# A sliding-window attention with a gated MLP on one Trainium2 core: w_out loaded four consecutive rows per partition, w_in's blocks read with a stride of four

## The chip, the cores and the metric

The kernel runs on one core of a Trainium2 chip. The metric is the device time of one execution in microseconds. The core has five engines, which run on their own instruction streams and wait for each other by semaphores: PE (matrix multiply; its weight loads are listed apart as PEld), DVE (vector), ACT (activations), POOL (GpSimd) and SP (which here only issues DMAs). POOL issues the DMAs that load and cast the inputs. A few DMAs more come from SP and one from ACT. 16 DMA engines carry all of them.

## The reference, cut to what matters

```python
# attention: 8 batches, 8 heads, 576 positions, head size 64
scores = q @ k.T / sqrt(64)                 # only 0 <= row - col < 64 is kept
attn = softmax(scores)                      # rows
x = (attn @ v) as (8 * 576, 512)            # 4608 tokens, heads side by side
# MLP
h = x @ w_in                                # 512 -> 2048
g = h * cos(h)
out = g @ w_out                             # 2048 -> 512, float32
```

The order of the 2048 inner units is free: any permutation of w_in's columns leaves the output as it is, if w_out's rows are permuted alike.

## The kernel before, in words

**Stages.** The 4608 tokens are cut into nine token tiles of 512 (`mt` 0 to 8). The MLP of tile `mt` runs on PE while the attention that feeds the next tiles is worked in between, on all engines. Each token tile has a first part, h = x w_in in 16 blocks of 128 inner units (`ff`), each of four matmuls over the four pieces of the model dimension (`ks`), and a second part, out = g w_out. ACT takes the sine of h (shifted by pi/2), DVE multiplies it by h. The last three tiles (6 to 8) do the second part with seven products of halves in place of eight, for which sums of quarters of w_out are made beforehand (`sum_weights`).

**The weights.** `w_in_sb` is one SBUF tile of 128 partitions by 4 x 2048 in bfloat16: partition p holds row `ks * 128 + p` of w_in for the four `ks`, 2048 columns each. Four DMAs load it (`load_w_in`, line 208; steps `Lwi.0` to `Lwi.3`): piece i brings columns 512 i to 512 i + 511 of all four `ks`. Block `ff` is columns 128 ff to 128 ff + 127, so blocks 0 to 3 need piece 0 alone, 4 to 7 piece 1, and so on. `w_out_sb` is 128 partitions by 16 blocks by 512: partition p of block ff holds row 128 ff + p. Four DMAs load it (`load_w_out`, line 211; steps `Lwo.0` to `Lwo.3`), each with four rows of 2 KB per partition, which lie 128 rows apart in DRAM.

**The order of the work.** Up to the end of token tile 0 the order is written out by hand in the string `FIRST` (lines 51 to 71): each word is one step, and a step's instructions go to their engines in that order. Behind that a plan of due times (`at`, `pump`) does it. Each engine runs its own instructions strictly in order. The piece of `FIRST` that the change touches is this:

```python
"... w.0.1 w.1.1 c.1.1.a i.3.1 h.0.0.1 h.0.1.4 "
"tb n.2.1.p c.0.1.d Lwi.3 w.2.1 h.0.2.0 n.3.1.p v.0.1 S.0.0 Gm.11 w.3.1 S.0.1 h.0.3.3 Lwo.0 ..."
```

`h.g.f.bank` is `first_half` (line 455): inner blocks 2f and 2f + 1 for half g (256 tokens) of token tile 0, thus eight matmuls of 128x256 on line 460, with `ks` running innermost. `w.p.g` is a transpose of softmax weights on PE (line 409), `n.p.g.p` their normalisation on POOL (line 393), `S` the sine on ACT, `v` the values matmuls on PE. `Lwi.0` to `Lwi.2` stand well ahead of this piece, `Lwi.3` stands in it, behind `h.0.0` and `h.0.1`. From token tile 1 on the first part is line 496 (`first`), with matmuls of 128x512; the second part is line 479 for token tile 0, 747 for tiles 1 to 5 and 585 for 6 to 8.

**The waits.** Nobody writes the semaphore waits by hand. The tile layer under the kernel records what each instruction reads and writes of which tile, in the order of the program, and gives an instruction a wait wherever it finds that its bytes may overlap those of an earlier writer (or, for a write, of an earlier reader) on another engine or a DMA. Software DMAs take eight semaphores in turn; the four loads of w_in have the numbers 6, 7, 0 and 1, and a load first waits for the former user of its semaphore.

Of the kernel before, what the change touches and what calls it, by code (L numbers as in the profile page):

```python
# [74 lines left out]
def kernel(  # L75
# [9 lines left out]
    nc = tc.nc  # L85
# [5 lines left out]
    n_ff = d_ff // 128  # L91
# [14 lines left out]
    w_in_sb = const.tile([128, PAIRS, d_ff], BF16, name="w_in")  # L106
    w_out_sb = const.tile([128, n_ff, d_model], BF16, name="w_out")
    w_in_v = moe_w_in.rearrange("(a p) f -> p a f", p=128)
    w_out_v = moe_w_out.rearrange("(a p) f -> p a f", p=128)
    ident = const.tile([128, 128], BF16, name="ident")  # L110
    mask = const.tile([128, 3, 128], F32, name="mask")
    mask16 = const.tile([128, 6, 128], BF16, name="mask16")
# [4 lines left out]
    st = {}  # L117
# [3 lines left out]
    H_BANKS = [banks * 3 + [last] for *banks, last in (["O1", "X0", "X1", "S", "O0", "X0"], ["X1", "S", "X0", "O1", "O0", "S"])]  # L121
    BANKS = ("O1", "X0", "X1", "S", "O0")
    W_PARTS = 4
    half = MT // 2

    def bank(which, name):
        return ps.tile([128, 512], F32, tag=which, name=name)
# [53 lines left out]
    def load_chunk(name, b, c):  # L181
        if (name, b) not in st:
            st[name, b] = rows_tile(name)[:, 0:NB * d_model].rearrange("p (c x) -> p c x", c=NB)
        n = min(128, S - 128 * c)
        src = {"q": q, "k": k}[name][b, :, c * 128:c * 128 + n]
        nc.gpsimd.dma_start(out=st[name, b][0:n, c].rearrange("p (h d) -> p h d", h=H),  # L186
                            in_=src.rearrange("h p d -> p h d"))

    def load_v(b, c):
        n = 128 if c < 4 else 64  # L190
        vt = vtiles[b % 2][:n, 2 * c if c < 4 else 2 * c - 1]
        nc.gpsimd.dma_start(out=vt.rearrange("p (h d) -> p h d", h=H),  # L192
                            in_=v[b, :, c * 128:c * 128 + n, :].rearrange("h p d -> p h d"))
# [13 lines left out]
    def load_w_in(lo, hi):  # L207
        nc.gpsimd.dma_start(out=w_in_sb[:, :, lo:hi], in_=w_in_v[:, :, lo:hi])

    def load_w_out(lo, hi):  # L210
        nc.gpsimd.dma_start(out=w_out_sb[:, lo:hi], in_=w_out_v[:, lo:hi])

    def transposed(name, b, p):
        t_ps = ps_t.tile([128, S], BF16, tag="t", name=f"t{name}_ps")
# [240 lines left out]
    def first_half(g, f, which):  # L455
        st["h", g, f] = h_ps = bank(BANKS[which], "h_ps")
        for e in range(2):
            ff = 2 * f + e
            for ks in range(PAIRS):
                nc.tensor.matmul(out=h_ps[:, half * e:half * e + half], lhsT=w_in_sb[:, ks, ff * 128:ff * 128 + 128],  # L460
                                 rhs=st["xT", 0][:, ks, half * g:half * g + half], start=ks == 0, stop=ks == PAIRS - 1,
                                 skip_group_check=True)

# [10 lines left out]
    def second_part(q_, m, which=None):  # L474
        if q_ == 0:
            st["out", m] = bank(BANKS[which], "out_ps")
        n = n_ff // W_PARTS
        for ff in range(n * q_, n * q_ + n):
# [14 lines left out]
    def first(mt, ff, ks, start, stop):  # L493
        if start:
            st["h", ff] = bank(H_BANKS[mt == 1][ff], "h_ps")
        nc.tensor.matmul(out=st["h", ff], lhsT=w_in_sb[:, ks, ff * 128:ff * 128 + 128],  # L496
                         rhs=st["xT", mt][:, ks], start=start, stop=stop)

    def skewed(mt, ks, n):
        for ff in range(SKEW):  # L500
            first(mt, ff, ks, n == 0, n == PAIRS - 1)
# [107 lines left out]
    for i, (b, jobs, banks) in enumerate(bursts):  # L609
        t = T * (b - 1)  # L610
# [55 lines left out]
    for n in range(16):  # L666
        i, f = divmod(n, 4)
# [14 lines left out]
    def spread_first(lo, hi):  # L682
# [5 lines left out]
             "Lq1": lambda p: load_heads("q", 1, p, 1), "Lk1": lambda p: load_heads("k", 1, p, 1),  # L688
             "Lv0": lambda c: load_v(0, c), "Lv1": lambda c: load_v(1, c), "Lq2": lambda c: load_chunk("q", 2, c), "Lk2": lambda c: load_chunk("k", 2, c),
             "Lwi": lambda i: load_w_in(i * d_ff // W_PARTS, (i + 1) * d_ff // W_PARTS),  # L690
             "Lwo": lambda i: load_w_out(i * n_ff // W_PARTS, (i + 1) * n_ff // W_PARTS),
             "io": put_steps, "mk": put_masks, "mc": cast_masks,
             "tq": lambda p: tr_q(0, p), "tk": lambda p: tr_k(0, p), "Tq": lambda p: tr_q(1, p), "Tk": lambda p: tr_k(1, p),
             "pq": lambda p, engine: put_q(0, p, engine), "pk": lambda p, engine: put_k(0, p, engine),
# [6 lines left out]
             "n": lambda p, g, engine: g_norm(2 * p + g, engine), "w": lambda p, g: g_trans(2 * p + g),  # L701
             "c": lambda p, g, engine: g_put(2 * p + g, engine), "v": values_half, "x": put_x_half,
             "tb": sine_table, "tb2": exp_table, "h": first_half, "S": sine_half, "g": gate_half,
             "Gs": g_scores, "Gm": g_max, "Ge": g_exp, "Gi": g_inv, "Gn": g_norm, "Gw": g_trans, "Gc": g_trans,
             "Gp": g_put, "V": lambda p: values(1, p), "X": lambda p, engine: put_x(1, p, engine),
# [7 lines left out]
    for mt in range(1, n_mt):  # L713
# [7 lines left out]
        for ff in range(n_ff):  # L721
            for ks in range(PAIRS):
                if ff >= SKEW:
                    first(mt, ff, ks, ks == 0, ks == PAIRS - 1)
            h_ps = st.pop(("h", ff))
            sin = moe.tile([128, MT], F32, tag="sin", name="sin", bufs=4)
            if ff % 2 == 0:
                gt = moe.tile([128, 2, MT], BF16, tag="gT", name="gT", bufs=n_ff // 2 + 2)
                gT.append(gt)
            e = ff % 2  # L730
            nc.scalar.activation(sin, h_ps, AF.Sin, bias=math.pi / 2.0)  # L731
            if ff == n_ff - 1 and mt < B:
                exp_table()
            nc.vector.tensor_tensor(out=gt[:, e], in0=h_ps, in1=sin, op=ALU.mult)  # L734
            pump(base + ff)
# [51 lines left out]
```

## Time and profile before

| what | value |
|---|---|
| runs of the kernel before | 299.11, 299.21, 297.6 us (median 299.11) |
| the profiled execution's own time | 296.92 us |
| its span in the profile | 295.2 us |
| PE busy | 285.3 us, 97% of the span |
| PEld busy (beside PE) | 163.2 us |
| DVE, ACT, POOL busy | 230.3, 238.0, 209.7 us |
| software DMA queue | 100896 packets, 18.06 MB written |
| granted TensorE clock | 1.0 |

All times below are us from the start of the span. A matmul's duration in the profile holds its latency (379 ns for 128x512); in a row of matmuls one starts much sooner than the former ends, so how fast a row goes is read from its length by its count. In the tables of waits an engine's idle time is put down to what ended it. A DMA's "us to landing" is from its issue.

### The profile page before, as it was taken

How to read it: one execution, taken by the hardware profiler on the slowest of the kernel's cores; microseconds unless marked ns; L12 is line 12 of the kernel's file. 1: busy time of each engine (PE TensorE's matmuls, PEld its weight loads, DVE VectorE, ACT ScalarE, POOL GpSimd, SP SyncE). 2: the span in 40 equal slices, each digit the busy share in tenths (PEclk: the TensorE clock that was granted, in tenths of full speed). 3: DMA queues.
4: the chain of work that ended last, by engine and by line, in shares of the span. 5: the costliest groups of instructions: out<-in, count | busy, mean ns of one | idle time of the engine just before them, and what ended most of it. 6: DMA issues, size and time to landing. Idle time of an engine off the chain costs nothing.

```text
span 295.2 us, 8262 instructions
## 1 busy us (share of the span) xinstructions
PE 285.3 (97%) x2786; PEld 163.2 (55%) x2815; DVE 230.3 (78%) x906; ACT 238.0 (81%) x791; POOL 209.7 (71%) x230
## 2 busy tenths in 40 slices
PE   8979999999999999999999999999999999999995
PEld 3668854544454444444454545444547854884595
DVE  4998888887887876788678876996689878957853
ACT  5998699888987798879987999799977896937710
POOL 9999568992899759984999399948995476133200
PEclk9999999999999999999999999999999999999999
DMA  7999999999999999999999999999959415042013
GB/s 149 174 201 205 196 191 143 141 143 155 203 197 120 162 235 154 155 163 232 168 142 158 235 155 145 147 213 185 141 122 200 45 38 178 2 117 83 0 38 107
DMA packets 168267, 43.81 MB, mean 148 GB/s; under 512 B 155616, under 2 KB 163872, under 8 KB 168224
## 3 DMA queue, kind: packets, MB, share of 16 engines
q0 software_dynamic: 100896, 18.06, 83.5%
q1 hardware_dynamic: 67184, 25.15, 46.7%
q8 instruction: 22, 0.36, 0.5%
q14 instruction: 21, 0.17, 0.2%
q10 hardware_dynamic: 144, 0.07, 0.1%
HBM read 36.70 MB, written 9.44 MB: 156 GB/s over the span
## 4 chain that ended last, share of the span: by engine, by line
PE 86%; POOL 5%; ACT 3%; DMA 2%; issue 2%; DVE 1%; POOLq 0%
PE h_ps L496 38%; PE out_ps L747 18%; PE out_ps L585 13%; PE h_ps L460 5%; PE out_ps L479 5%; PE o_ps L428 3%; ACT e L376 2%; PE s_ps L327 2%; DMA wT<-w 2%; POOL v L192 1%; POOL q L169 1%; POOL k L169 1%; POOL w L393 1%; PE tw_ps L409 1%; PE s_ps L349 1%
## 5 line engine op out<-in xcount | busy, mean ns | idle before, releaser
L496 PE MATMUL h_ps<-xT,w_in 128*128 128x512 bf16 x502 | 111.3, 379 | 1.3 <-DVE xT L130 0.8
L393 POOL TENSOR_TENSOR w<-e,rden 128x512 bf16<-128x512 f32 (+1 forms) x68 | 69.2, 1030 | 48.6 <-DVE rden L386 38.6
L734 DVE TENSOR_TENSOR gT<-h_ps,sin 128x512 bf16<-128x512 f32 x128 | 84.6, 687 | 21.8 <-ACT sin L731 20.4
L376 ACT ACTIVATE e<-s,negm 128x128 f32<-128x128 f32 (+1 forms) x256 | 97.2, 382 | 2.6 <-DVE negm L364 1.6
L731 ACT ACTIVATE sin<-h_ps 128x512 f32<-128x512 f32 x128 | 73.6, 599 | 25.4 <-PE h_ps L496 23.5
L496 PEld LDWEIGHTS <-w_in 128*128 128x128 bf16 x512 | 50.2, 98 | 59.3
L747 PE MATMUL out_ps<-w_out,gT 128*128 128x512 bf16 x305 | 68.7, 379 | 1.1 <-issue 0.8
L364 DVE CUSTOM_DVE_ANT_0 s<-s_ps,mask 128x128 f32<-128x128 f32 (+1 forms) x256 | 55.8, 277 | 1.9 <-PE s_ps L349 1.6
L747 PEld LDWEIGHTS <-gT 128*128 128x128 bf16 x320 | 30.4, 98 | 35.5
L376 ACT ACTIVATION_READ_ACCUMULATOR e<-s,negm 128x1 f32 x256 | 48.0, 188 | 0.0
L192 POOL DMA_DIRECT2D v<-in_v_dram x40 | 34.1, 874 | 1.0 <-issue 0.9
L186 POOL DMA_DIRECT2D q<-in_q_dram x30 | 26.3, 894 | 3.6 <-issue 3.0
L186 POOL DMA_DIRECT2D k<-in_k_dram x30 | 26.3, 887 | 0.0
L386 DVE RECIPROCAL rden<-den 128x4 f32<-128x4 f32 (+1 forms) x73 | 12.0, 165 | 17.2 <-ACT e L376 16.8
L130 POOL COPY v<-v 64x1536 bf16<-64x1536 bf16 (+3 forms) x16 | 22.9, 1431 | 0.4
L364 DVE DVE_READ_ACCUMULATOR2_ANT negm<- 128x1 f32 x256 | 21.2, 83 | 0.0
L525 POOL TENSOR_TENSOR qT<-gT 128x512 bf16<-128x512 bf16 x12 | 13.6, 1154 | 9.1 <-DVE gT L734 9.0
L130 DVE CAST xT<-o_ps 128x512 bf16<-128x512 f32 x24 | 15.5, 680 | 5.8 <-PE o_ps L428 5.5
L585 PEld LDWEIGHTS <-gT 128*128 128x128 bf16 x152 | 14.0, 98 | 2.2
L460 PE MATMUL h_ps<-xT,w_in 128*128 128x256 bf16 x128 | 14.6, 273 | 0.0
L479 PE MATMUL out_ps<-w_out,gT 128*128 128x512 bf16 x60 | 14.3, 380 | 0.3 <-issue 0.2
L556 DVE TENSOR_TENSOR out_sb<-out_ps,p 128x512 f32<-128x512 f32 (+2 forms) x16 | 8.6, 548 | 6.7 <-ACT p L130 5.6
(90 smaller groups left out, 327.0 us busy)
## 6 DMA issues: line engine op xcount, KB each, us to landing
out_dram<-out_sb SPq DMA_DIRECT2D x16, 512.0 KB, 8.2
v<-in_v_dram POOLq DMA_DIRECT2D x32, 128.0 KB, 5.8
q<-in_q_dram POOLq DMA_DIRECT2D x24, 128.0 KB, 8.5
k<-in_k_dram POOLq DMA_DIRECT2D x24, 128.0 KB, 7.1
w_in<-in_moe_w_in_dram POOLq DMA_DIRECT2D x4, 512.0 KB, 9.4
w_out<-in_moe_w_out_dram POOLq DMA_DIRECT2D x4, 512.0 KB, 11.0
q<-in_q_dram POOLq DMA_DIRECT2D x7, 144.0 KB, 5.7
k<-in_k_dram POOLq DMA_DIRECT2D x7, 144.0 KB, 5.8
```

The lines of the kernel that those rows point to most:

```text
L130: {"a": nc.scalar.copy, "p": nc.gpsimd.tensor_copy}.get(engine, nc.vector.tensor_copy)(out, in_)
L186: nc.gpsimd.dma_start(out=st[name, b][0:n, c].rearrange("p (h d) -> p h d", h=H), in_=src.rearrange("h p d -> p h d"))
L192: nc.gpsimd.dma_start(out=vt.rearrange("p (h d) -> p h d", h=H), in_=v[b, :, c * 128:c * 128 + n, :].rearrange("h p d -> p h d"))
L364: nc.vector.tensor_tensor_reduce(out=s[:, u, c], in0=s_ps[:, u, c], in1=mask[:, 2 - j % 2 if j else 0, c], scale=-scale if b else -1.0, sc ...
L376: nc.scalar.activation(e[:, u, c], s[:, u, c], AF.Exp, bias=negm[:, u:u + 1], scale=1.0 if n < n_first else -1.0, accum_out=den[:, u:u + 1])
L393: (nc.gpsimd if engine == "p" else nc.vector).tensor_tensor(out=w[:, 0:u], in0=e[:, 0:u], op=ALU.mult, in1=rden[:, 0:u].unsqueeze(2).to_br ...
L460: nc.tensor.matmul(out=h_ps[:, half * e:half * e + half], lhsT=w_in_sb[:, ks, ff * 128:ff * 128 + 128], rhs=st["xT", 0][:, ks, half * g:ha ...
L496: nc.tensor.matmul(out=st["h", ff], lhsT=w_in_sb[:, ks, ff * 128:ff * 128 + 128], rhs=st["xT", mt][:, ks], start=start, stop=stop)
L585: nc.tensor.matmul(out=to[n_] if split else to[:, e], lhsT=lhs[name][f // 2][:, f % 2, 128 * e:128 * e + 128], rhs=rhs[name][:, f, lo:hi], ...
L731: nc.scalar.activation(sin, h_ps, AF.Sin, bias=math.pi / 2.0)
L734: nc.vector.tensor_tensor(out=gt[:, e], in0=h_ps, in1=sin, op=ALU.mult)
L747: nc.tensor.matmul(out=o_ps[e], lhsT=gT[ff // 2][:, ff % 2, ms * 128:ms * 128 + 128], rhs=w_out_sb[:, ff], start=ff == 0, stop=ff == n_ff - 1)
```

## The change

`load_w_out` takes a piece number and loads rows 512 i to 512 i + 511, with four consecutive rows (8 KB of DRAM in one run) to each partition: partition p of group i holds rows 512 i + 4 p to 512 i + 4 p + 3. Block ff = 4 i + a thus holds the inner units 512 i + 4 p + a. To match, the new `w_in_block` reads w_in for block ff as every fourth column of its group: columns 512 i + a, 512 i + a + 4, and so on, 128 of them. What is stored of w_in, the loads `Lwi`, the number, order and sizes of matmuls, and the second part's reads of w_out are as before. All line numbers behind the new function are five higher in the changed kernel.

```diff
@@ -106,7 +106,6 @@
-    w_out_v = moe_w_out.rearrange("(a p) f -> p a f", p=128)
@@ -121,6 +120,7 @@
     W_PARTS = 4
+    w_out_v = moe_w_out.rearrange("(g p a) f -> g p a f", p=128, a=n_ff // W_PARTS)
@@ -207,8 +207,13 @@
-    def load_w_out(lo, hi):
-        nc.gpsimd.dma_start(out=w_out_sb[:, lo:hi], in_=w_out_v[:, lo:hi])
+    def load_w_out(i):
+        n = n_ff // W_PARTS
+        nc.gpsimd.dma_start(out=w_out_sb[:, n * i:n * i + n], in_=w_out_v[i])
+
+    def w_in_block(ks, ff):
+        n = n_ff // W_PARTS
+        return w_in_sb[:, ks].rearrange("p (g t a) -> p g a t", t=128, a=n)[:, ff // n, ff % n]
@@ -457,7 +462,7 @@
-                nc.tensor.matmul(out=h_ps[:, half * e:half * e + half], lhsT=w_in_sb[:, ks, ff * 128:ff * 128 + 128],
+                nc.tensor.matmul(out=h_ps[:, half * e:half * e + half], lhsT=w_in_block(ks, ff),
@@ -493,7 +498,7 @@
-        nc.tensor.matmul(out=st["h", ff], lhsT=w_in_sb[:, ks, ff * 128:ff * 128 + 128],
+        nc.tensor.matmul(out=st["h", ff], lhsT=w_in_block(ks, ff),
@@ -688,7 +693,7 @@
-             "Lwo": lambda i: load_w_out(i * n_ff // W_PARTS, (i + 1) * n_ff // W_PARTS),
+             "Lwo": load_w_out,
```

The instructions stand in the same order on every engine. What the built program has otherwise is some waits. Here are three places of the two builds, with the waits in brackets: DMASW6, 7, 0 and 1 are the semaphores of w_in's pieces 0, 1, 2 and 3, PE that of PE's own progress.

PE, the beginning of `h.0.0`, the first use of w_in (`w` is the softmax weights, `h_ps` the product's bank). Before:

```order
L409 MATMUL tw_ps<-ident,w 128x128
L460 LDWEIGHTS w_in [waits DMASW6_49]
L460 MATMUL h_ps<-xT,w_in 128x256
L460 LDWEIGHTS w_in
L460 MATMUL h_ps<-xT,w_in 128x256
```

And changed:

```order
L414 MATMUL tw_ps<-ident,w 128x128
L465 LDWEIGHTS w_in [waits DMASW6_49]
L465 MATMUL h_ps<-xT,w_in 128x256
L465 LDWEIGHTS w_in [waits DMASW7_49,DMASW0_49]
L465 MATMUL h_ps<-xT,w_in 128x256
```

The waits for pieces 1 and 2 stood at blocks 4 and 8 (the beginnings of `h.0.2` and `h.0.4`); they now stand at the second weight load of block 0.

PE, the beginning of `h.0.2`, behind the transposes of `w.2.1`. Before:

```order
L409 LDWEIGHTS w
L409 MATMUL tw_ps<-ident,w 128x128
L460 LDWEIGHTS w_in [waits DMASW7_49]
L460 MATMUL h_ps<-xT,w_in 128x256 [waits DVE_49]
L460 LDWEIGHTS w_in
L460 MATMUL h_ps<-xT,w_in 128x256
```

And changed:

```order
L414 LDWEIGHTS w
L414 MATMUL tw_ps<-ident,w 128x128
L465 LDWEIGHTS w_in
L465 MATMUL h_ps<-xT,w_in 128x256 [waits DVE_49]
L465 LDWEIGHTS w_in [waits DMASW1_49]
L465 MATMUL h_ps<-xT,w_in 128x256
```

The wait for piece 3 stood at block 12 (the beginning of `h.0.6`); it now stands at the second weight load of block 4.

POOL, from the third load of w_in to the first of w_out (`w<-e,rden` are the normalisations). Before:

```order
L208 DMA w_in<-in_moe_w_in_dram 128x4x512 [waits DMASW0_49]
L393 TENSOR_TENSOR w<-e,rden 128x512 [waits DVE_49,Pool_49]
L393 TENSOR_TENSOR w<-e,rden 128x512
L393 TENSOR_TENSOR w<-e,rden 128x512 [waits DVE_49] x5
L208 DMA w_in<-in_moe_w_in_dram 128x4x512 [waits DMASW1_49]
L393 TENSOR_TENSOR w<-e,rden 128x512 [waits DVE_49]
L211 DMA w_out<-in_moe_w_out_dram 128x4x512 [waits DMASW2_49,PE_49]
```

And changed:

```order
L208 DMA w_in<-in_moe_w_in_dram 128x4x512 [waits DMASW0_49]
L398 TENSOR_TENSOR w<-e,rden 128x512 [waits DVE_49,Pool_49]
L398 TENSOR_TENSOR w<-e,rden 128x512
L398 TENSOR_TENSOR w<-e,rden 128x512 [waits DVE_49] x5
L208 DMA w_in<-in_moe_w_in_dram 128x4x512 [waits DMASW1_49,PE_49]
L398 TENSOR_TENSOR w<-e,rden 128x512 [waits DVE_49]
L212 DMA w_out<-in_moe_w_out_dram 128x2048 [waits DMASW2_49]
```

The load of piece 3 has a wait for PE that it did not have: for the matmuls of `h.0.0` and `h.0.1`, which stand ahead of it in `FIRST` and read w_in. The first load of w_out, behind it, needs none of its own for PE any more.

## The prediction

> **What bounds the kernel now.** I read the chain of waits on the page first, since it says whose work sets the end:
>
> ```profile
> PE 86%; POOL 5%; ACT 3%; DMA 2%; issue 2%; DVE 1%; POOLq 0%
> ```
>
> It is PE, and by one count almost without a hole. The windows view for the stretch from the first inner blocks to the last matmul:
>
> ```profile
> 23.40:292.00 268.60, 265.21 (x2430) 149.97 (x2457) 212.18 (x845) 218.79 (x713) 187.98 (x197) 1.00 1.32 146
> ```
>
> PE is busy for 265.21 of 268.60 us. So there are 268.60 - 265.21 = 3.4 us in all that any easing of DMAs or POOL could win behind 23.4, and whatever holds PE up there goes into the end in full, since no slack takes it in. PE's instructions run in the order in which they stand, so a held weight load holds everything behind it.
>
> Next the chain in order of time and the timeline of POOL, around the two places where waits have moved (start, length, what):
>
> ```profile
> 21.42 1.75 PE h_ps L460 x16
> 23.16 0.22 PE tw_ps L409 x4
> 23.39 0.87 PE h_ps L460 x8
> 24.26 0.17 issue
> ...
> 26.44 10.59 PE h_ps L460 x96
> ```
>
> ```profile
> 13.74 0.74 POOL L208 DMA_DIRECT2D w_in<-in_moe_w_in_dram  x1 [0.27 <-DVE rden L386]
> ...
> 22.17 0.81 POOL L208 DMA_DIRECT2D w_in<-in_moe_w_in_dram  x1
> 22.99 1.05 POOL L393 TENSOR_TENSOR w<-e,rden 128x512 bf16<-128x512 f32 x1
> 23.99 0.80 POOL L211 DMA_DIRECT2D w_out<-in_moe_w_out_dram  x1
> ...
> 31.94 0.74 POOL L211 DMA_DIRECT2D w_out<-in_moe_w_out_dram  x1 [2.08 <-DMA w_out<-in_moe_w_out_dram]
> 32.72 3.32 POOL L192 DMA_DIRECT2D v<-in_v_dram  x4
> 39.01 1.77 POOL L186 DMA_DIRECT2D q<-in_q_dram  x2 [2.97 <-issue]
> ```
>
> The x16 at 21.42 are `h.0.0` and `h.0.1`, the x8 at 23.39 are `h.0.2`, each matmul 1.75 / 16 = 0.11 us. The third piece of w_in is issued at 13.74, the fourth at 22.17. Now how long they take to land; the DMA view, asked for the moment of each of four issues, gives in turn the third piece, the fourth, the first load of w_out, and the first software load of the program, which finds an empty queue:
>
> ```profile
> w_in<-in_moe_w_in_dram POOLq DMA_DIRECT2D x1, 512.0 KB, 12.5
> w_in<-in_moe_w_in_dram POOLq DMA_DIRECT2D x1, 512.0 KB, 6.6
> w_out<-in_moe_w_out_dram POOLq DMA_DIRECT2D x1, 512.0 KB, 7.7
> q<-in_q_dram POOLq DMA_DIRECT2D x1, 144.0 KB, 4.4
> ```
>
> The third piece lands at 13.74 + 12.5 = 26.24, the fourth at 22.17 + 6.6 = 28.77. Today this hurts nobody: blocks 8 and 9 of `h.0.4`, the first to need the third piece, begin at 26.4, and those of `h.0.6` later still.
>
> **The change part by part.** *The wait for pieces 1 and 2 at block 0.* The second weight load of `h.0.0` now wants the third piece, so its matmul, at 21.42 + 0.11 = 21.5 before, comes after 26.24. The lag from a landing to the instruction that it frees is read at POOL: the first w_out lands at 23.99 + 7.7 = 31.69, and the load that waits for its semaphore starts at 31.94, so 0.25. PE goes on at 26.5. That is 5.0 us of stall; the size is firm, as nothing ahead of 21.4 is changed. The 15 matmuls that are left end at 23.16 + 5.0 = 28.2.
>
> *The wait for PE at piece 3, and for piece 3 at block 4.* POOL reaches this load at 22.2, as before, but must hold it until `h.0.1` is done: 28.2. Then PE, after one matmul of `h.0.2`, stands until it has landed. Its landing is bounded by 4.4 (a load of about a quarter of the bytes in an empty queue) and 6.6 (the same load with a piece ahead of it). I take 6.2: the empty-queue load with its own transfer taken off, plus that of a piece. The own transfer I put at the pace at which POOL issues such loads, 0.67 (the row below); a piece costs 28.77 - 26.24 = 2.5 behind another. So 4.4 - 0.67 + 2.5 = 6.2. It is at the upper end because the row of 6.6 is the same load and the other one is much smaller.
>
> ```profile
> L169 POOL DMA_DIRECT2D k<-in_k_dram x7 | 4.7, 665 | 0.0
> ```
>
> So piece 3 lands at 28.2 + 6.2 = 34.4, PE goes on at 34.65, and the second matmul of `h.0.2` was at 23.39 + 0.11 = 23.5. Both stalls together are 34.65 - 23.5 = 11.15 us, with 9.35 and 11.55 as bounds.
>
> Behind POOL's held load are queued the last normalisation of that group (1.05), the four loads of w_out, and the loads of q, k and v for the next batch. They start at 28.2 + 0.8 = 29.0 instead of 22.99, 6.0 late; who needs them on PE is 11 late itself, so they gain 5 us of room and hold up nobody. What is given back: the hole of 0.17 at 24.26 closes, as the work in it has long been done; I count 0.2, and at most 1.0 of the 3.4.
>
> *A cold restart.* PE will stand for 5.0 and about 6 us. What that does to its speed afterwards no row behind the start shows: the longest wait of PE there is 1.06 (for POOL's w, at 16.65). But the program's first matmuls, which follow on idleness, are slow:
>
> ```profile
> L137 PE MATMUL busy<-w_out x11: 389/634/634, 1.2 to 7.4; 128*128 128x512 bf16 x11
> ...
> 1.20 3.60 PE L137 MATMUL busy<-w_out 128*128 128x512 bf16 x8 [1.20 <-DVE small L678]
> 16.65 0.62 PE L409 MATMUL tw_ps<-ident,w 128*128 128x128 bf16 x8 [1.06 <-POOL w L393]
> ...
> 87.01 10.74 PE h_ps L496 x49
> ```
>
> 634 ns each and (3.60 - 0.634) / 7 = 0.42 us apart, where the same shape later goes at 10.74 / 49 = 0.22. Eight of them thus lost 3.60 - 8 x 0.22 = 1.8 us. If both stalls leave PE cold, the 15 matmuls between them double (1.6 us) and the second restart costs 1.8, together 3.4; if none does, 0. I take one restart, 1.8: each stall is four times the wait after which PE is still quick, but how long an idleness it takes no row says. [...]
>
> *The strided weight loads.* 640 weight loads of w_in now take every fourth column.
>
> ```profile
> L496 PEld LDWEIGHTS <-w_in 128*128 128x128 bf16 x512 | 50.2, 98 | 59.3
> L460 PEld LDWEIGHTS <-w_in 128*128 128x128 bf16 x128 | 12.3, 98 | 1.4
> ...
> 18.72 0.23 PEld L409 LDWEIGHTS <-w 128*128 128x128 bf16 x4 [0.55 <-POOL w L393]
> ```
>
> The matmul of the step before hides each: 0.11 us on line 460, 0.22 on line 496. Of the same size, four packed loads take 0.23, so they follow at (0.23 - 0.098) / 3 = 0.044 us. A strided load may thus take two and a half times as long and cost nothing. At four times, 0.176, line 460 would pay 128 x (0.176 - 0.11) = 8.4 us and line 496 still nothing. No row here has a strided one; a gain is excluded, as the packed one is hidden already. I take 0, because the cover is so wide, and keep 8.4 as a rival. [...]
>
> *w_out in pieces of 8 KB.* POOL's issue may get cheaper, and the landings earlier.
>
> ```profile
> L211 POOL DMA_DIRECT2D w_out<-in_moe_w_out_dram x4 | 3.1, 771 | 2.2 <-DMA w_out<-in_moe_w_out_dram 2.1
> L192 POOL DMA_DIRECT2D v<-in_v_dram x40 | 34.1, 874 | 1.0 <-issue 0.9
> ```
>
> 128 pieces instead of 512: by the nearest rows, 665 ns for loads of fewer pieces than w_out's and 874 for more, four issues move by -0.4 to +0.4 us. POOL's idle 2.97 ahead of 39.01 covers that, and PE first wants w_out at 37.9 plus 11. Without that cover it would be those 0.4. I count 0.
>
> **The sum.** 296.92 (the profiled execution, of which 295.2 are span) + 11.15 - 0.2 + 1.8 = 309.7. The median of the runs is 299.11, 2.2 above the profiled one, so for a median I say 299.11 + 12.75 = 311.9 us, 4.3% slower.
>
> **The rivals.** *Faster:* the waits are met when PE comes to them, and the lighter w_out takes PE's holes away. Its place is the stretch from 24 to 56 us, its price at most the 3.4 us: 295.7. It decides only if the third piece is there by 21.4 and the fourth by 23.5. Against it: the row of 12.5 puts the third at 26.24, and the fourth isn't even issued before `h.0.1` ends.
>
> *No change:* both semaphores have been passed by other loads that share them, so the waits don't hold. Then 299. For it: the semaphores are shared by turns. Against it: they count up, and the value waited for includes the piece itself.
>
> *Weight loads, too:* the stalls and the 8.4 us: 320. For it only that no row shows such a load.
>
> *The pieces of 8 KB are cut up again,* so that w_out comes as before. It changes nothing in the time, since PE doesn't wait for w_out.
>
> **How the numbers follow.** A measurement of this kernel can tell about 0.5% from no change. Stalls as computed: 0.87. Stalls and dear weight loads: 0.06. No change: 0.04. Faster: 0.03. Within the likeliest, the lower end has the landing of 4.4 (-1.8), no cold restart (-1.8), 1.0 given back (-0.8) and the profiled execution's level: 309.7 - 4.4 = 305.3; the upper end has 6.6 (+0.4) and both restarts (+1.6): 313.9. I say 305 to 316, stretched a little toward the dear loads. Faster 0.03, same 0.04, slower 0.93.
>
> **What would show it.** In the profile after: PE idle at about 21.5 to 26.5 and 28.5 to 34.6, put down to DMA w_in; POOL's fourth load of w_in at 28.2 instead of 22.17; matmuls on line 465 at 273 ns again, and some of them longer just behind the stalls (cold); from `h.0.3` on PE as full as before. Wrong would be: PE going on through 21.5 without a wait, weight loads of w_in well above 98 ns with the rows on line 465 at more than 0.11 us apart, or the stalls there but the end less than 9 us later.

## The result, and the profile after

| | before | changed |
|---|---|---|
| median of the runs | 298.38 us (297.6 to 299.21, 4 runs) | 311.41 us (310.58 to 311.56, 4 runs) |
| profiled execution, own time | 296.92 us | 311.5 us |
| span | 295.2 us | 309.7 us |

The changed kernel is slower: 1.0434 times the time before, with a 95% interval of 1.0399 to 1.0468. The loss is 13.0 us by the medians and 14.6 by the two profiled executions.

The chain of waits on the page of the changed kernel, by engine and by line:

```profile
PE 83%; DMA 9%; ACT 3%; POOL 3%; issue 1%; DVE 0%; POOLq 0%
PE h_ps L501 36%; PE out_ps L752 18%; PE out_ps L590 12%; DMA w_in<-in_moe_w_in_dram 6%; PE h_ps L465 5%; PE out_ps L484 5%; PE o_ps L433 3%; ACT e L381 2%; PE s_ps L332 2%; DMA wT<-w 2%; DMA q<-in_q_dram 2%; POOL v L192 1%; PE s_ps L354 1%; PE tw_ps L414 1%; POOL w_in L208 0%
```

A link that wasn't there has come in: the DMA of w_in, 6% of the span, in a kernel that PE bounded all through. Where it sits, the chain in order of time shows (start, length, what):

```profile
14.54 12.56 DMA w_in<-in_moe_w_in_dram
27.10 0.05 issue
27.14 3.40 PE h_ps L465 x15
30.54 0.29 issue
30.84 5.44 DMA w_in<-in_moe_w_in_dram
36.28 0.05 issue
36.33 1.68 PE h_ps L465 x7
...
40.71 10.60 PE h_ps L465 x96
51.31 0.38 PE tk_ps L230 x12
```

The row x15 holds the matmuls of `h.0.0` and `h.0.1` behind the first one, the row x7 those of `h.0.2` behind its first. Each stands behind a transfer: x15 behind the third piece, issued at 14.54, and x7 behind the fourth, issued at 30.84. PE's and POOL's timelines name the same two waits, from PE's side and from POOL's:

```profile
22.02 0.27 PE L465 MATMUL h_ps<-xT,w_in 128*128 128x256 bf16 x1
27.14 3.39 PE L465 MATMUL h_ps<-xT,w_in 128*128 128x256 bf16 x15 [4.85 <-DMA w_in<-in_moe_w_in_dram]
...
36.33 1.68 PE L465 MATMUL h_ps<-xT,w_in 128*128 128x256 bf16 x7 [5.16 <-DMA w_in<-in_moe_w_in_dram]
```

```profile
30.84 0.81 POOL L208 DMA_DIRECT2D w_in<-in_moe_w_in_dram  x1 [7.83 <-PE h_ps L465]
```

POOL sat for 7.83 us with the fourth load in its hands, waiting for the matmuls of `h.0.1`; PE then waited for this very load. The DMA view gives its landing from issue:

```profile
w_in<-in_moe_w_in_dram POOLq DMA_DIRECT2D x1, 512.0 KB, 5.4
```

The third thing is the pace. In the windows view, the column behind POOL's is the granted clock of PE:

```profile
20.00:28.00 8.00, 3.10 (x64) 2.29 (x59) 4.49 (x35) 4.64 (x13) 2.53 (x3) 0.88 0.77 147
28.00:36.00 8.00, 3.17 (x17) 2.06 (x15) 0.42 (x1) 1.19 (x2) 5.15 (x7) 0.50 0.50 76
36.00:44.00 8.00, 7.67 (x82) 6.45 (x83) 4.11 (x7) 3.38 (x6) 5.70 (x9) 0.77 1.26 190
44.00:52.00 8.00, 8.00 (x103) 7.81 (x101) 6.74 (x11) 5.50 (x11) 2.65 (x3) 1.00 1.44 195
```

From 28 to 36 the clock is 0.50. The 0.77 of the next row is a mean over 8 us; shorter windows show where it comes back:

```profile
36.00:39.60 3.60, 3.27 (x31) 2.32 (x32) 0.45 (x2) 0.60 (x1) 1.98 (x5) 0.50 1.08 181
39.80:44.00 4.20, 4.20 (x52) 3.96 (x51) 3.46 (x6) 2.78 (x5) 3.52 (x5) 1.00 1.41 199
```

By windows of 0.1 us the clock fell at 26.05 and rose at 39.71, so it was down from the first stall until 3.4 us behind the second. The 15 matmuls behind the first stall take 3.40 us where before the 16 of the two groups took 1.75.

And the weight loads, which in both kernels are hidden behind matmuls (the rows of 128x512 in the first part run at 0.22 us a matmul in both, 10.74 us for 49 before and 13.83 us for 64 changed), and the issues of the two weight matrices:

```profile
L501 PEld LDWEIGHTS <-w_in 128*128 128x128 bf16 x512 | 57.9, 113 | 51.7
```

```profile
L208 POOL DMA_DIRECT2D w_in<-in_moe_w_in_dram x4 | 3.1, 778 | 8.6 <-PE h_ps L465 7.8 <-DVE negm L364 0.8
L212 POOL DMA_DIRECT2D w_out<-in_moe_w_out_dram x4 | 2.3, 572 | 1.6 <-DMA w_out<-in_moe_w_out_dram 1.6
```

A strided weight load takes 113 ns instead of 98; a load of w_out keeps POOL for 572 ns instead of 771.

### The profile page after: what moved, and what is told of

Read it like the earlier page. It is cut to its first block, busy times and chain, and to the rows that moved or that the text cites. A ratio compares the mean times of both kernels' runs of the same rounds, so it can differ in the third digit from the quotient of the medians.

```text
span 309.7 us, 8289 instructions
## 1 busy us (share of the span) xinstructions
PE 291.9 (94%) x2815; PEld 174.0 (56%) x2815; DVE 231.0 (75%) x906; ACT 238.7 (77%) x791; POOL 209.2 (68%) x230
## 2 busy tenths in 40 slices
DMA packets 166731, 43.81 MB, mean 141 GB/s; under 512 B 155616, under 2 KB 161824, under 8 KB 166688
## 4 chain that ended last, share of the span: by engine, by line
PE 83%; DMA 9%; ACT 3%; POOL 3%; issue 1%; DVE 0%; POOLq 0%
PE h_ps L501 36%; PE out_ps L752 18%; PE out_ps L590 12%; DMA w_in<-in_moe_w_in_dram 6%; PE h_ps L465 5%; PE out_ps L484 5%; PE o_ps L433 3%; ACT e L381 2%; PE s_ps L332 2%; DMA wT<-w 2%; DMA q<-in_q_dram 2%; POOL v L192 1%; PE s_ps L354 1%; PE tw_ps L414 1%; POOL w_in L208 0%
## 5 line engine op out<-in xcount | busy, mean ns | idle before, releaser
L736 ACT ACTIVATE sin<-h_ps 128x512 f32<-128x512 f32 x128 | 73.7, 600 | 25.2 <-PE h_ps L501 23.6
L501 PEld LDWEIGHTS <-w_in 128*128 128x128 bf16 x512 | 57.9, 113 | 51.7
L752 PE MATMUL out_ps<-w_out,gT 128*128 128x512 bf16 x320 | 72.0, 380 | 0.0
L752 PEld LDWEIGHTS <-gT 128*128 128x128 bf16 x320 | 30.4, 98 | 35.5
L465 PE MATMUL h_ps<-xT,w_in 128*128 128x256 bf16 x128 | 17.9, 303 | 10.0 <-DMA w_in<-in_moe_w_in_dram 10.0
L471 ACT ACTIVATE sin<-h_ps 128x512 f32<-128x512 f32 x16 | 9.6, 597 | 16.5 <-PE h_ps L465 16.5
L465 PEld LDWEIGHTS <-w_in 128*128 128x128 bf16 x128 | 14.7, 120 | 12.0 <-DMA w_in<-in_moe_w_in_dram 10.6
L130 DVE COPY wT<-tw_ps 128x512 bf16<-128x512 bf16 (+1 forms) x12 | 4.7, 407 | 14.7 <-PE tw_ps L414 14.6
```

What stands on the lines that cost most here:

```text
L130: {"a": nc.scalar.copy, "p": nc.gpsimd.tensor_copy}.get(engine, nc.vector.tensor_copy)(out, in_)
L501: nc.tensor.matmul(out=st["h", ff], lhsT=w_in_block(ks, ff), rhs=st["xT", mt][:, ks], start=start, stop=stop)
L752: nc.tensor.matmul(out=o_ps[e], lhsT=gT[ff // 2][:, ff % 2, ms * 128:ms * 128 + 128], rhs=w_out_sb[:, ff], start=ff == 0, stop=ff == n_ff - 1)
```

## The experiments

The theory is the prediction's: the loss comes from three waits in the built program, plus cold restarts of PE. The waits are PE's for pieces 1 and 2 at block 0, the fourth load's for PE, and PE's for piece 3 at block 4. The strided reads and the large pieces of w_out cost nothing in themselves. The rivals: the strided loads make PE slow; the loads of w_out help or hinder. All ratios are to the kernel before, run on the same chip; the numbers in brackets are 95% intervals.

**One tile of w_in for each load** (`e1_tiles`). It keeps strided reads and 8 KB pieces, and takes away what can be mistaken for an overlap:

```diff
-    w_in_sb = const.tile([128, PAIRS, d_ff], BF16, name="w_in")
+    w_in_sb = [const.tile([128, PAIRS, d_ff // 4], BF16, name=f"w_in{i}") for i in range(4)]
-        nc.gpsimd.dma_start(out=w_in_sb[:, :, lo:hi], in_=w_in_v[:, :, lo:hi])
+        nc.gpsimd.dma_start(out=w_in_sb[lo * W_PARTS // d_ff], in_=w_in_v[:, :, lo:hi])
-        return w_in_sb[:, ks].rearrange("p (g t a) -> p g a t", t=128, a=n)[:, ff // n, ff % n]
+        return w_in_sb[ff // n][:, ks].rearrange("p (t a) -> p a t", a=n)[:, ff % n]
```

> The changed kernel with w_in held in four SBUF tiles, one for each load, instead of one; strided reads and 8 KB pieces of w_out stay. A weight load can then only wait for the load of its own tile. Waits theory (the stalls come from waits for w_in's later pieces, and from the fourth load's wait for PE): as the kernel before, ratio to it 0.995 to 1.005, no PE idle for DMA w_in, fourth load of w_in at about 22 again. Strided-loads theory (reading w_in with a stride makes PE slow): the stalls go, but the ratio stays at 1.01 or more, with matmuls on the first part more than 0.115 us apart for half token tiles.

Measured: 297.84 us, ratio 0.9992 [0.9965, 1.0019]. In the built program the waits for the four pieces are back at blocks 0, 4, 8 and 12. PE's timeline at the former place of the first stall, and the weight loads of this kernel:

```profile
21.26 1.91 PE L465 MATMUL h_ps<-xT,w_in 128*128 128x256 bf16 x16
23.01 0.39 PE L414 MATMUL tw_ps<-ident,w 128*128 128x128 bf16 x4
23.60 1.06 PE L465 MATMUL h_ps<-xT,w_in 128*128 128x256 bf16 x8 [0.21 <-DMA w_in<-in_moe_w_in_dram]
```

```profile
L465 PEld LDWEIGHTS <-w_in 128*128 128x128 bf16 x128 | 13.7, 113 | 1.1 <-DMA w_in<-in_moe_w_in_dram 1.1
```

The 16 matmuls stand in one piece again, at the same pace as before, although each of their weight loads is strided and takes 113 ns. PE still waits for w_in, where none was expected, but 0.9 us in all, for the pieces that the blocks really need.

**The stride alone** (`e2_stride_only`), with w_out's rows loaded as before, so that the inner units and the rows of w_out don't match:

```diff
-    w_out_v = moe_w_out.rearrange("(g p a) f -> g p a f", p=128, a=n_ff // W_PARTS)
+    w_out_v = moe_w_out.rearrange("(g a p) f -> g p a f", p=128, a=n_ff // W_PARTS)
```

> w_in read with the stride as in the changed kernel, but w_out loaded as before (rows 128 apart), so that inner units and rows of w_out don't match and the output isn't the reference's. Waits theory: all of the loss is there, ratio 1.040 to 1.047, two PE stalls of about 5 us for DMA w_in. If the 8 KB pieces of w_out had a part in it: ratio below 1.035.

Measured: 310.55 us, ratio 1.0419 [1.037, 1.0467]. The loss is there without the pieces of 8 KB. The profiled execution is the quickest of its four, 308.24 us. Its second stall is 5.33 us; its first is shorter, and the 15 matmuls behind it are not slow, which is used further below:

```profile
26.32 1.83 PE L465 MATMUL h_ps<-xT,w_in 128*128 128x256 bf16 x15 [3.56 <-DMA w_in<-in_moe_w_in_dram]
```

**w_out alone** (`e3_w_out_only`), with w_in's blocks read as before, so that the two don't match either:

```diff
-        return w_in_sb[:, ks].rearrange("p (g t a) -> p g a t", t=128, a=n)[:, ff // n, ff % n]
+        return w_in_sb[:, ks, ff * 128:ff * 128 + 128]
```

> w_out loaded in 8 KB pieces as in the changed kernel, but w_in's blocks read contiguously as before, so that the output isn't the reference's. Waits theory: ratio 0.995 to 1.005, POOL's four issues about 0.2 us shorter each, nothing of it at the end. If lighter loads of w_out free PE: ratio below 0.995. If large pieces hold other loads up: above 1.005.

Measured: 298.0 us, ratio 0.9998 [0.9969, 1.0026]. POOL's issues are 568 ns each, thus 0.2 us shorter, and nothing of it reaches the end.

**The waits alone** (`e8_waits_only`). Here no load and no read of the kernel before is changed. Three small matmuls, which read every fourth column of w_in's piece 0, are put in, so that the built program gets the changed kernel's waits:

```diff
+    def touch():
+        ps_touch = ps_t.tile([128, MT], F32, tag="t", name="touch")
+        nc.tensor.matmul(out=ps_touch[:, 0:64], lhsT=w_in_sb[:, 1, 0:512:4], rhs=ident[:, 0:64], start=True, stop=True,
+                         skip_group_check=True)
-    ... i.3.1 h.0.0.1 h.0.1.4 tb n.2.1.p c.0.1.d Lwi.3 w.2.1 h.0.2.0 ...
+    ... i.3.1 wt h.0.0.1 h.0.1.4 wt tb n.2.1.p c.0.1.d Lwi.3 w.2.1 wt h.0.2.0 ...
```

> The kernel before, with packed weight loads and w_out as it was, plus three matmuls of 128x64 whose weights are every fourth column of piece 0 (result never read): ahead of h.0.0, behind h.0.1 and ahead of h.0.2. By them alone the built program has the changed kernel's waits at the same places: pieces 1 and 2 ahead of block 0, the fourth load behind h.0.1, piece 3 ahead of block 4. Waits theory: all of the loss with none of the changed loads, ratio 1.038 to 1.050. If the 640 strided loads or w_out have a part: clearly less than the changed kernel beside it.

Measured: 311.91 us, ratio 1.046 [1.0426, 1.0494], beside 311.29 us for the changed kernel on the same chip. Its PE timeline has the same two stalls, and its weight loads are packed:

```profile
26.62 0.24 PE L142 MATMUL touch<-ident,w_in 128*128 128x64 bf16 x1 [4.78 <-DMA w_in<-in_moe_w_in_dram]
26.68 3.60 PE L465 MATMUL h_ps<-xT,w_in 128*128 128x256 bf16 x16
...
36.14 0.24 PE L142 MATMUL touch<-ident,w_in 128*128 128x64 bf16 x1 [5.38 <-DMA w_in<-in_moe_w_in_dram]
```

```profile
L501 PEld LDWEIGHTS <-w_in 128*128 128x128 bf16 x512 | 50.1, 98 | 59.4
```

These four settle it from both sides: the edits without the waits (`e1_tiles`) cost nothing, the waits without the edits (`e8_waits_only`) cost all.

**The fourth load ahead** (`e4_piece_early`), to tell the two stalls apart:

```diff
-    "... e.3.0 Lwi.2 Tk.1 ..."       "... c.0.1.d Lwi.3 w.2.1 ..."
+    "... e.3.0 Lwi.2 Lwi.3 Tk.1 ..." "... c.0.1.d w.2.1 ..."
```

> The changed kernel with the fourth load of w_in issued right behind the third, ahead of all that reads w_in, so that it waits for nobody on PE. Waits theory: one stall instead of two, at the second weight load of block 0, until the fourth piece has landed at about 29 (2.5 us behind the third); PE is 7.5 us late there, and one cold restart costs 1.8: 9 us over the kernel before, ratio 1.027 to 1.034. If what counts is the number of bytes that are waited for and not the order: no better than the changed kernel, 1.043.

Measured: 306.73 us, ratio 1.029 [1.0256, 1.0325]. One stall is left, a little longer, as the fourth piece is behind the third in the queue:

```profile
28.84 3.36 PE L465 MATMUL h_ps<-xT,w_in 128*128 128x256 bf16 x15 [5.61 <-DMA w_in<-in_moe_w_in_dram]
```

The circle, in which the fourth load waits for PE and PE for the fourth load, is thus worth some 4.6 us of the 13 by the medians; the first stall's growth is already taken off. In this profiled execution the clock was at 0.50 ahead of `h.0.0` too, from 17.37 to 20.78, so its places in time are not set beside those of the others.

**Each load cut into four** (`e7_loads_per_row_block`), one for each `ks`, in the one tile:

```diff
-        nc.gpsimd.dma_start(out=w_in_sb[:, :, lo:hi], in_=w_in_v[:, :, lo:hi])
+        for ks in range(PAIRS):
+            nc.gpsimd.dma_start(out=w_in_sb[:, ks, lo:hi], in_=w_in_v[:, ks, lo:hi])
```

> The changed kernel with each load of w_in cut into four, one for each ks, so that what a load writes is one contiguous run per partition, in the same single tile. Extent theory (the tile layer gives the needless waits because a load of four runs and a strided read are compared by their ends, not by their elements): no PE stall of 5 us at 22 and 30 any more, PE stays warm, the strided reads notwithstanding. But POOL issues 12 loads more, about 0.6 us each, 9 of them ahead of the normalisations at 14.5 that PE waits for: 5 us late there, ratio 1.010 to 1.025. If stride in a read alone gives the waits: stalls and ratio as in the changed kernel or worse.

Measured: 305.36 us, ratio 1.0255 [1.0228, 1.0281]. The waits are as the extent theory has them: in the built program every strided weight load waits for its own piece alone, and the loads of the fourth group do not wait for PE. The trace bears the latter out, as POOL issues them from 30.16 on, while `h.0.1` is still running. That the matmuls run through says less, since PE comes to them 8 us later than before:

```profile
23.42 1.04 PE L415 MATMUL tw_ps<-ident,w 128*128 128x128 bf16 x8 [7.79 <-POOL w L399]
...
29.36 1.91 PE L466 MATMUL h_ps<-xT,w_in 128*128 128x256 bf16 x16
```

The price is a little above what was expected: PE waits 7.79 us for POOL instead of the 5 estimated. Besides the longer row of issues, POOL stands for 2.4 us between them, put down to earlier DMAs, whose semaphores the loads share. And PE is cold afterwards: the clock is at 0.50 from 17.89 to 28.13. So this gives the right waits, but at a price.

**Fillers in the stalls** (`e5_fill`, and again as `e10_fill_again`), to measure the cold restarts:

```diff
+    def fill(n):
+        ps_fill = ps_t.tile([128, MT], F32, tag="t", name="fill")
+        for _ in range(n):
+            nc.tensor.matmul(out=ps_fill, lhsT=ident, rhs=mask16[:, 0:4].rearrange("p u c -> p (u c)"), start=True, stop=True,
+                             skip_group_check=True)
-    ... h.0.0.1 h.0.1.4 tb n.2.1.p c.0.1.d Lwi.3 w.2.1 ...
+    ... fl.20 h.0.0.1 h.0.1.4 tb n.2.1.p c.0.1.d Lwi.3 fl.22 w.2.1 ...
```

> The changed kernel with 20 idle matmuls of 128x512 (identity by the mask, result never read) on PE ahead of h.0.0 and 22 behind the fourth load of w_in, 4.3 and 4.8 us of work that lies inside the two stalls of 4.85 and 5.16. Cold-restart theory (the matmuls behind the stalls are slow because PE stood idle): the rows on the first part of token tile 0 are 0.11 us apart throughout, granted clock 1.0, and some 3.3 us come back: ratio to the kernel before 1.030 to 1.035. If they are slow because of the strided loads or of the transfers beside them: slow rows as in the changed kernel and 1.043 or more.

Measured: 309.05 us, ratio 1.0411 [1.0352, 1.047], a miss, as the whole interval lies above the 1.030 to 1.035 expected, and too wide to tell the theories apart, while its profiled execution (308.22 us, clock 1.0) was 3.3 us below that of the changed kernel. So it was run again with more runs and the changed kernel (`e9_changed_again`) beside it:

> The changed kernel itself, on the same chip as the fillers and the waits alone, as the mark for both: ratio 1.040 to 1.047 by its first measurement.

> The kernel with fillers in the stalls once more, since its first measurement was too wide to tell 1.032 from 1.043. Cold-restart theory: 3 us (1.0 percentage points) below the changed kernel beside it, the difference of the two traces. If the traces differed by chance: no difference.

Measured: the changed kernel 311.29 us, 1.0447 [1.0418, 1.0475]; with fillers 308.2 us, 1.0338 [1.0311, 1.0366]. PE does 42 matmuls more (the trace lists 40 of them) and the kernel is 3.1 us faster than the changed one:

```profile
21.08 4.48 PE L143 MATMUL fill<-mask,ident 128*128 128x512 bf16 x19
25.40 0.27 PE L471 MATMUL h_ps<-xT,w_in 128*128 128x256 bf16 x1
26.59 1.83 PE L471 MATMUL h_ps<-xT,w_in 128*128 128x256 bf16 x15 [0.91 <-DMA w_in<-in_moe_w_in_dram]
```

The 15 matmuls take 1.83 us instead of 3.39, behind the landing of the same piece, and the clock is 1.00 throughout.

**Bursts of weight loads** (`e6_burst`), which measure the disputed load by itself: five times 64 short matmuls at the end of the kernel before, of this form, with `0:256:2`, `0:512:4`, `0:1024:8` and `0:2048:16` after the packed one:

```diff
+    few = dict(out=ps_burst[:, 0:64], rhs=ident[:, 0:64], start=True, stop=True, skip_group_check=True)
+    for i in range(64):
+        nc.tensor.matmul(lhsT=w_in_sb[:, i % 4, 0:128], **few)
```

> The kernel before with five bursts of 64 matmuls of 128x64 behind its last product (result never read), whose weights are 128 columns of w_in, packed, every 2nd, 4th, 8th and 16th; the matmuls are so short that the weight load sets the pace. Cover theory (a load of every fourth column costs too little to be seen): at every 4th the pace is at most 0.09 us, twice the packed one. If a strided load falls to a fourth of the speed: 0.15 us or more, which would be seen on the 0.11 us matmuls.

One execution was measured; here is its PE timeline, one row for each step from packed to every 16th:

```profile
292.26 2.03 PE L761 MATMUL burst<-ident,w_in 128*128 128x64 bf16 x64
294.13 2.03 PE L763 MATMUL burst<-ident,w_in 128*128 128x64 bf16 x64
296.00 2.30 PE L765 MATMUL burst<-ident,w_in 128*128 128x64 bf16 x64
298.13 4.15 PE L767 MATMUL burst<-ident,w_in 128*128 128x64 bf16 x64
302.12 4.11 PE L769 MATMUL burst<-ident,w_in 128*128 128x64 bf16 x64
```

From start to start by 64: 29, 29, 33 and 62 ns for every column, every 2nd, 4th and 8th. The two 29 are an upper bound for the load: 64 columns of a matmul take 27 ns by an estimate from this kernel's pace (10.74 us for 49 of 512 columns, in the prediction), so there the matmul may set the pace. At every fourth the pace is 33 ns, under a matmul of 110 at least. (The kernel's 308.98 us hold the bursts themselves.)

## Why the prediction was right, point by point

It said 311.9 us and slower; measured were 311.41. That the two are so close is luck in part: the sum starts from a median of 299.11 where the four runs of the kernel before have a median of 298.38, and its 12.75 us of loss stand against 13.0. By the profiled execution it said 309.7, and 311.5 was measured. The mechanism is the one that was predicted. The two profiled executions let each term be set beside its size, by the moments at which PE reaches the same instruction:

| PE's place | before | changed | later by |
|---|---|---|---|
| first matmul of `h.0.0` | 21.25 | 22.02 | 0.77 |
| end of `h.0.1` | 23.16 | 30.54 | 7.38 |
| second matmul of `h.0.2` | 23.33 | 36.33 | 13.00 |
| end of token tile 0's first part | 37.03 | 51.31 | 14.28 |
| end of the last matmul | 291.99 | 306.55 | 14.56 |

(The prediction has 23.5 for the third place, from the chain, whose pieces start where the former one ends; the timeline has the eight matmuls start at 23.22. The same holds for its 21.5. Both stalls together would be 0.17 us longer by it.)

*The wait at block 0.* Said: 5.0 us, PE going on at 26.5, the size firm. Measured: 4.85 idle, PE going on at 27.14. This execution was late by 0.77 already at 22.02, its third load being issued at 14.54 instead of 13.74. That is nothing of the change: the changed kernel's other profiled execution (`e9_changed_again`) starts `h.0.0` at 21.41. But there PE goes on at 27.20, after 5.49 idle, and in the run of the stride alone at 26.32, after 3.56. So the place is right and the size is not firm: it moves by 2 us from one execution to another, and that 4.85 comes near 5.0 is chance.

*The circle of the fourth load.* Said: a landing of 6.2 and 6.15 us of further delay. Measured: a landing of 5.4 and 13.00 - 7.38 = 5.62 us. The DMA engines were idle when it was issued, as said: they moved no packet from 29 to 31 us. The landing lay midway between the two rows that bounded it, 0.8 under the 6.2 that was added up. POOL let go of the load at 30.84, not 28.2, as the late start of this execution and the first cold restart came before it.

*The cold restart* was the term that was sized worst: 1.8 for one of two, and PE was cold behind both stalls. Between the first two places PE lost 7.38 - 0.77 - 4.85 = 1.76 us besides the idleness. From the third to the fourth it lost 14.28 - 13.00 = 1.28 and the 0.17 of a hole that closed, thus 1.45. Together that is 3.2, and by the fillers 3.1. The prediction's 3.4 for both was the right one of its ends. The landing (0.8 too long) and the restart (1.4 too short) made up for each other in part, so the sum is better than its terms.

The prediction asked how long an idleness it takes. The length of the stall alone doesn't decide it. In the run of the stride alone the clock stayed at 1.00 behind 3.56 us, but earlier in the same execution it fell behind a wait of 1.26:

```profile
17.15 0.74 PE L414 MATMUL tw_ps<-ident,w 128*128 128x128 bf16 x8 [1.26 <-POOL w L398]
```

```profile
14.11:17.52 3.41, 1.92 (x43) 1.48 (x44) 2.80 (x7) 3.41 (x17) 3.35 (x5) 1.00 2.07 172
17.52:20.93 3.41, 3.41 (x42) 2.38 (x41) 3.00 (x10) 2.66 (x16) 3.41 (x4) 0.50 1.24 208
24.34:27.75 3.41, 1.43 (x13) 1.44 (x14) 0.76 (x8) 1.89 (x3) 0.00 (x0) 1.00 0.33 58
27.75:31.17 3.42, 0.73 (x9) 0.50 (x7) 0.42 (x1) 0.76 (x2) 2.71 (x4) 1.00 0.32 33
31.17:34.58 3.41, 0.77 (x4) 0.58 (x5) 0.00 (x0) 0.00 (x0) 3.41 (x5) 0.50 1.21 183
```

These windows are laid in steps of 3.41 us from the moments at which the clock changed in that execution (17.52, 20.93, 31.17), which are 3.41 us apart, and three times that. The first number behind the comma is PE's busy time. The stall of 3.56 us, from 22.75 to 26.32, is parted by 24.34, and PE worked 1.43 us in the window that holds the rest of it; the clock stayed. PE's busy time in such a window doesn't decide it alone either: the clock fell behind windows in which PE was busy for 1.92 and for 0.73 us, though it stayed behind one with 1.43. What does decide it, these runs leave open. Each of the stalls of 4.78 to 5.61 us met slow matmuls behind it; a shorter one may or may not, as the waits of 1.26 and 3.56 us show.

*Given back.* Said: 0.2 us. The hole of 0.17 did close, but PE's delay grows by another 0.28 from the end of the first part to the last matmul, so nothing of it is left at the end. That POOL and the loads are not late for anybody was right.

*Strided weight loads.* Said: 0, covered up to two and a half times the packed load. The load grew to 113 ns (98 before), and its pace is 33 ns by the bursts, against 29 at most; nothing of it is seen in the ratio 0.9992. At every eighth column the bursts' pace is 62 ns; why the step from 33 to 62 lies there, no run here shows.

*w_out.* Said: POOL's issues between -0.4 and +0.4 us in all, nothing at the end. Measured: 4 x (771 - 572) = 0.8 us less on POOL, more than the bound, as both rows that gave it were of loads with more than 128 pieces; nothing at the end, 0.9998. The large pieces weren't cut up again: the page counts 2048 packets under 2 KB fewer (161824 against 163872), and 1536 fewer in all (166731 against 168267), so 512 came in for the 2048.

*The rivals.* No change by semaphores passed early: both waits held, with 4.85 and 5.16 us of idle PE ahead of them. Dear weight loads: shown not to be so, by `e1_tiles` (0.9992). Faster: with the waits away, what is left of the change gains nothing that can be measured.

What the tile layer does is shown as far as this: with a load that writes four runs per partition in the same tile, a strided read gets waits for loads whose elements it doesn't touch; with one run per load, or a tile per load, it doesn't; a packed read doesn't either. That it compares ends instead of elements in such a case is the simplest reading of that, not more. It fits that the first strided load of block 0 (`ks` 0) got no needless wait: its columns end ahead of the first element of every later piece.

## What to carry to other kernels

A change of a read's pattern can change the waits, even where no instruction moves: look at the waits of the built program around every tile that is filled by several loads, and give each load its own tile before reading across it with a stride. A load that stands in program order behind reads of the same tile can be made to wait for them, and the next read for the load: such a circle costs a whole transfer, 5.4 us from issue to landing here. And behind the two stalls of PE here, 4.85 and 5.16 us, the cold clock cost some 1.8 and 1.5 us more; a shorter one can bring it as well: the clock fell behind a wait of 1.26 us, and stayed up behind one of 3.56 (`e2_stride_only`). Idle matmuls that nobody reads won that back here: 3.1 us for the two stalls.

## What the runs showed of the hardware that was not expected

In the bursts (`e6_burst`) the pace of 128-column weight loads is 29 ns at most for every and every 2nd bfloat16 column, 33 for every 4th, and 62 at every eighth, where it stays at every sixteenth (64 in 4.11 us, against 4.15 at every eighth).

The fourth load of w_in, 512 KB in POOL's queue, landed 5.4 us after its issue when the DMA engines were idle at that moment (no packet from 29 to 31 us), where before, behind other loads (245 GB/s from 22 to 23 us), it took 6.6.

And the granted clock of PE changed in steps, between 1.00 and 0.50. These are the moments of its changes between 12 and 56 us, from windows of 0.1 us, in the six kept traces that have any:

| run | falls and rises in turn, us | time between them, us |
|---|---|---|
| the changed kernel | 26.05, 39.71 | 13.66 |
| `e2_stride_only` | 17.52, 20.93, 31.17, 38.00 | 3.41, 10.24, 6.83 |
| `e4_piece_early` | 17.37, 20.78, 27.61, 34.44 | 3.41, 6.83, 6.83 |
| `e7_loads_per_row_block` | 17.89, 28.13 | 10.24 |
| `e8_waits_only` | 24.54, 31.36, 34.78, 41.60 | 6.82, 3.42, 6.82 |
| `e9_changed_again` | 24.29, 31.12, 34.53, 41.36 | 6.83, 3.41, 6.83 |

Every time between two changes is one, two, three or four times 3.41 to 3.42 us, while the moments themselves lie otherwise in each execution. The same kernel was cold without a break from its first stall to behind its second in one execution, and warm for 3.41 us in between in the other.
